# Products of zeros on TensorE in the idle time of its plan: into a spare bank up to the first block, into an open accumulator later

## The chip, the cores and the metric

The kernel runs on one core of a Trainium2 chip. The metric is the device time of one execution in microseconds (us); lower is better. TensorE does the matrix products, VectorE (DVE in the profile), ScalarE (ACT) and GpSimd (POOL) the rest, and SyncE (SP) issues the loads and stores.

## What is computed

Three stages follow each other: an attention by landmarks, a channel mixer behind a Fourier transform, and a gated mixer.

```python
q_lm = q.reshape(B, H, m, S // m, D).mean(axis=3)        # B 8, H 8, S 576, D 64, m 32
k_lm = k.reshape(B, H, m, S // m, D).mean(axis=3)
A, Bm, C = sm(q, k_lm), sm(q_lm, k_lm), sm(q_lm, k)      # sm: scaled softmax of a @ b.T
Z = Bm.T / (norm1(Bm) * norminf(Bm) + 1e-06)
for _ in range(6):
    Z = 2 * Z - Z @ Bm @ Z
x = A @ Z @ C @ v                                        # then heads side by side: 8 x 576 x 512
u = x + real(fft(fft(x, axis=1), axis=2))
un = (u - mean(u)) / sqrt(var(u) + 1e-06)
x = u + np.maximum(un @ w_ch1, 0.0) @ w_ch2              # 512 -> 2048 -> 512
xk, xr = mixes of x and of x one token back
k = np.maximum(xk @ w_k, 0.0)
out = sigmoid(xr @ w_r) * (k * k @ w_v)                  # 512 -> 1024 -> 512, 512 -> 512
```

## The kernel before

The tokens (8 batches of 576) are cut into nine blocks of 512 (`BLK`, `NB`). `phase1` (line 544) does the attention and the transform of one batch: `landmarks`, `chain_b` (with its `series` of six steps on the tiles `RX` and `bdR`), `chain_c`, `chain_a`, `tail`. Its products are small and mostly float32, and go into PSUM banks named `gp`. `norm` (line 1058) normalizes one block; its first two blocks take the sums of squares by 16 products of one column each, `one` with `tmp`, issued in two passes (x32 in the trace). `block_a` (line 1127) is the channel mixer of one block. Its `first(f)` (line 1133) makes 12 products of 512 columns into one of two banks `ph` and its `second(f)` (line 1148) makes 12, three each into four accumulators `acc`, banks 0 to 3, that stay open from f = 0 to f = 15. The order is first(0), then first(f), second(f-1) in turn, then second(15). The class `Gated` (after the loop at line 1187) does the third stage in the same way.

Each weight comes as 64-bit floats and is turned into two float16 halves on chip by `Weights.run`: three ScalarE steps and three VectorE steps on `wbits` or `more`, then a high half on ScalarE (`w1h`, `w2h`) and a low half on VectorE (`w1l`, `w2l`). Those of `block_a` are 32 pieces, put in among the batches and the first blocks.

Nothing is issued as the program text stands. Every call records an `Op` (line 128) with a cost in us, and `Plan.issue` (line 365) simulates the engines: each Op starts when its engine is free and its operands are there (with `HOP`, 0.2 us, from engine to engine), the one with the largest key (its path to the end plus its `lead`) first. PSUM banks are handed out in the same simulation by `grant` (line 421): `fixed` (line 387) holds the banks that are bound to `acc` and `ph` from the time that their first product could start, and `gp` takes any other. The order found is then issued engine by engine and stays as it is. A product costs its columns divided by 2400 plus 0.0025 us in the plan (line 315), float32 four times that and 0.17 at least, so the plan has TensorE at its higher clock all the time. The products of `block_a` and `Gated` have `chain=True`: they keep the order in which they were recorded.

Of the kernel before, what the change touches and what calls it, by code (L numbers as in the profile page):

```python
# [11 lines left out]
F32 = mybir.dt.float32  # L12
F16 = mybir.dt.float16
# [36 lines left out]
def wide(x):  # L50
    return int(np.prod(x.shape[1:]))


class Ref:


    def __init__(self, tile, view, path=()):
        self.tile, self.view, self.path = tile, view, path
        self.shape, self.dtype = view.shape, view.dtype
# [68 lines left out]
class Op:  # L128
    def __init__(self, index, eng, run, cost, port=False, nbytes=0):
        self.index, self.eng, self.run, self.cost = index, eng, run, cost  # L130
        self.port, self.nbytes = port, nbytes
        self.preds, self.succs = set(), []
        self.tail = self.lead = self.est = self.end = 0.0
        self.group = self.last = None

NOW, START, CONVERT, SOON = 1000.0, 400.0, 170.0, 200.0


class Engine:
# [44 lines left out]
class Plan:  # L187
# [6 lines left out]
    def __init__(self, nc, shadow):  # L194
        self.nc, self.shadow = nc, shadow
        self.ops, self.groups = [], []
        self.slots, self.turn = {}, {}
        self.lead = self.slack = 0.0
        self.chained, self.count = None, 0
        self.v = Engine(self, nc.vector, "v")  # L200
        self.s = Engine(self, nc.scalar, "s")
        self.g = Engine(self, nc.gpsimd, "g")
# [112 lines left out]
    def mm(self, out, lhsT, rhs, start, stop, chain=False, **kw):  # L315

        cost = wide(rhs) / 2400.0 + 0.0025
        if rhs.dtype == F32:
            cost = max(4 * cost, 0.17)
        share = 4 if wide(lhsT) <= 32 else 2 if wide(lhsT) <= 64 else 1  # L320

        def run():
            self.nc.tensor.matmul(  # L323
                out.real(), lhsT=lhsT.real(), rhs=rhs.real(), start=start, stop=stop, **kw
            )

        op = self.record("pe", run, cost / share, [out], [lhsT, rhs])
        if chain:
            op.lead = 0.0
            if self.chained:  # L330
                op.preds.add(self.chained)
            self.chained = op

    def tr(self, out, in_, ident):
        def run():
            self.nc.tensor.transpose(out.real(), in_.real(), ident.real())  # L336

        self.record("pe", run, 0.108, [out], [in_, ident])
# [26 lines left out]
    def issue(self):  # L365
        ops = self.ops
        for g in self.groups:
            if g.group[0].bank is None:
                g.preds = self.outside(g)
            else:  # L370
                g.preds = g.group[0].ops[0].preds - {g}
        for op in ops:
            for p in op.preds:
                p.succs.append(op)
        for op in reversed(ops):
            cost = op.cost + (op.nbytes / 340e3 + 2.0 if op.nbytes else 0.0)
            op.tail = cost + max([
                s.tail + (self.HOP if s.eng != op.eng and op.eng else 0.0) for s in op.succs
            ] or [0.0])
            op.key = op.tail + op.lead  # L380
        left = {op: len(op.preds) for op in ops}
        free = dict(pe=0.0, v=0.0, s=0.0, g=0.0, sp=0.0)
        later = {e: [] for e in free}
        avail = {e: [] for e in free}
        pending, order = [], []
        bank = {n: 0.0 for n in range(8)}
        fixed, holds = set(), {}
        port = dma = 0.0

        def ready(op):  # L390
            op.est = max(
                [0.0]
                + [
                    p.end + (self.HOP + op.slack if p.eng and p.eng != op.eng else 0.0)
                    for p in op.preds
                ]
            )
            if op.group:
                first = min((o for t in op.group for o in t.ops), key=lambda o: o.index)
                op.est = max([0.0] + [p.end for p in first.preds if p is not op])  # L400
                op.key = first.key
                pending.append(op)
                if op.group[0].bank is not None:
                    fixed.add(op.group[0].bank)
            elif op.eng is None:
                done(op, op.est)
            else:
                heapq.heappush(later[op.eng], (op.est, op.index, op))

        def done(op, end):  # L410
            op.end = end
            for t in holds.pop(op, ()):
                t.left -= 1
                if t.left == 0:
                    bank[t.bank] = max(o.end for o in t.ops) + self.HOP
            for s in op.succs:
                left[s] -= 1
                if left[s] == 0:
                    ready(s)

        def grant():

            best = None
            wanted = sorted(pending, key=lambda g: -g.key)
            for k, g in enumerate(wanted):
                if g.group[0].bank is not None:
                    got = [g.group[0].bank]
                else:
                    got = sorted(
                        (b for b in bank if b not in fixed and bank[b] < np.inf),  # L430
                        key=lambda b: bank[b],
                    )[:len(g.group)]
                    if len(got) < len(g.group):
                        continue
                t = max([g.est] + [bank[b] for b in got])
                if t < np.inf and (best is None or t < best[0]):
                    best = t, g, got
            return best

        for op in ops:  # L440
            if not op.preds:
                ready(op)
        while len(order) < sum(op.eng is not None for op in ops):
            when = []
            for e in free:
                if avail[e]:
                    when.append((free[e], e))
                elif later[e]:
                    when.append((max(free[e], later[e][0][0]), e))
            g = grant()  # L450
            if g and (not when or g[0] <= min(when)[0]):
                t, op, got = g
                pending.remove(op)
                for x, b in zip(op.group, got):
                    x.bank, x.left = b, len(x.ops)
                    bank[b] = np.inf
                    for o in x.ops:
                        holds.setdefault(o, []).append(x)
                done(op, t)
                continue  # L460
            t, e = min(when)
            while later[e] and later[e][0][0] <= t:
                x = heapq.heappop(later[e])[2]
                heapq.heappush(avail[e], (-x.key, x.index, x))
            op = heapq.heappop(avail[e])[2]
            start = max(t, port) if op.port else t
            free[e] = end = start + op.cost
            if op.port:
                port = end
            if op.nbytes:  # L470
                dma = max(dma, end) + op.nbytes / 340e3
                end = dma + 2.0
            op.begin = start
            order.append(op)
            done(op, end)
        self.order, self.span = order, max(op.end for op in order)
        for op in order:
            op.run()
# [477 lines left out]
def build(nc, tc, a):  # L956
    shadow = bacc.Bacc("TRN2", target_bir_lowering=False, num_devices=1)
    iss = Plan(nc, shadow)
    v_, s_, g_ = iss.v, iss.s, iss.g
    mm, tr = iss.mm, iss.tr  # L960
    stack, pa_stack, p1_stack = ExitStack(), ExitStack(), ExitStack()
    with stack, tc.manual_schedule():
        ps_pool = Pool(stack, tc, "ps", space=PSUM)
        com = Pool(stack, tc, "com")
# [28 lines left out]
        one = iss.tile(com, [128, 1], F32, "one")  # L993
        v_.memset(one, 1.0 / DM)
        ones = one.to_broadcast([128, 128])
        w1 = [iss.tile(pa, [128, 4, FF1], F16, f"w1{x}") for x in "hl"]
        w2 = [iss.tile(pa, [128, 16, DM], F16, f"w2{x}") for x in "hl"]
        weights = Weights(iss, com)
# [128 lines left out]
        def block_a(i, un):  # L1127
            u = ub[i]
            acc = acc_banks()
# [18 lines left out]
            def second(f):  # L1148
                h = hs.pop(f)
                for m in range(4):  # L1150
                    sl = slice(128 * m, 128 * m + 128)
                    for n, (x, y) in enumerate(PARTS):
                        mm(
                            acc[m], w2[x][:, f, sl], h[:, y], f == 0 and n == 0,
                            f == 15 and n == 2, chain=True,
                        )

            first(0)
            for f in range(1, 16):
# [167 lines left out]
        for n in range(8 * NB + 2):  # L1327
            i, f = divmod(n, 8)
# [96 lines left out]
```

## Time and profile before

| | |
|---|---|
| median of 3 runs | 1582.57 us (1581.19 to 1584.06) |
| the profiled execution | 1584.5 us, span 1582.7 us |
| TensorE busy | 1529.7 us, 97% of the span |
| VectorE, ScalarE, GpSimd busy | 883.9 us (56%), 600.5 us (38%), 288.4 us (18%) |
| mean granted TensorE clock | 0.978 |

The granted clock is the share of full speed that the chip lets TensorE have; it has two levels here, 1.00 (2.4 GHz) and 0.50 (1.2 GHz), and a window over both shows a mean. A busy TensorE is not always a fast one: at the lower level a product is busy for twice the time. "Idle before" in a timeline is the time in which the engine had nothing running ahead of that instruction, and the name behind the arrow is what ended it.

### The profile page before, as it was taken

To read this page: it belongs to the slowest core of one execution; us is meant where nothing else is said; L and a number is where in the kernel's file an instruction comes from. 1 tells how busy PE (TensorE), PEld (TensorE's weight loads), DVE (VectorE), ACT (ScalarE), POOL (GpSimd) and SP (SyncE) were. 2 spreads that over 40 slices of the span, in tenths; PEclk is the share of its full clock that TensorE was granted. 3 is DMA by queue.
4 is the path that set the end of the run, shared out by engine and by line. 5 is a ranking of instruction groups with operands and counts; after the bars stand their busy time and mean duration, and the time that the engine had idled before them with its cause. 6 is when DMAs were issued, how large, how long until landed. Compare 5 with 4: busy or idle time off the path is not lost.

```text
span 1582.7 us, 20918 instructions
## 1 busy us (share of the span) xinstructions
PE 1529.7 (97%) x8182; PEld 784.4 (50%) x8182; DVE 883.9 (56%) x1802; ACT 600.5 (38%) x1233; POOL 288.4 (18%) x347
## 2 busy tenths in 40 slices
PE   6879899999999999999999999999999999999998
PEld 5535455555564554554544444444444444444443
DVE  6798887776764764634515344211587766643222
ACT  4465654444433433322312123111655544443221
POOL 2012020221210210210102012000454533221100
PEclk8788899999999999999999999999999999999999
DMA  7243414132322222100002200000121011000000
GB/s 272 67 133 121 134 55 152 38 115 76 100 71 81 86 72 80 61 1 28 1 0 80 107 28 0 27 0 28 53 80 54 27 54 54 28 1 27 27 28 27
DMA packets 43587, 97.87 MB, mean 62 GB/s; under 512 B 4064, under 2 KB 9440, under 8 KB 42976
## 3 DMA queue, kind: packets, MB, share of 16 engines
q1 hardware_dynamic: 43488, 96.53, 17.8%
q8 instruction: 65, 1.06, 0.3%
q14 instruction: 34, 0.28, 0.1%
HBM read 72.39 MB, written 24.12 MB: 61 GB/s over the span
## 4 chain that ended last, share of the span: by engine, by line
PE 93%; DVE 4%; ACT 1%; issue 1%; DMA 0%; SPq 0%; POOL 0%; ACTq 0%; DVEq 0%
PE ph L323 35%; PE acc L323 35%; PE gp L323 21%; PE gp L336 2%; DVE wbits L180 1%; DVE more L180 0%; DVE small L180 0%; DMA k<-in_k 0%; DVE uc L180 0%; DVE w1l L180 0%; DVE h L180 0%; ACT h L180 0%; DVE d L180 0%; DVE un L180 0%; DVE w2l L180 0%
## 5 line engine op out<-in xcount | busy, mean ns | idle before, releaser
L323 PE MATMUL ph<-un,w1h 128*128 128x512 f16 x1152 | 353.6, 382 | 10.6 <-DVE bst L180 6.1
L323 PE MATMUL acc<-h,w2h 128*128 128x512 f16 x1152 | 350.8, 382 | 1.2 <-ACT w2h L180 1.2
L180 DVE SCALAR_TENSOR_TENSOR h<-ph,h 128x512 f16<-128x512 f32 x144 | 99.3, 690 | 283.2 <-ACT h L180 282.4
L180 ACT ACTIVATE h<-ph 128x512 f16<-128x512 f32 x144 | 85.9, 597 | 379.2 <-PE ph L323 378.7
L323 PE MATMUL acc<-h,w2l 128*128 128x512 f16 x576 | 219.8, 382 | 4.3 <-DVE w2l L180 4.3
L323 PE MATMUL ph<-un,w1l 128*128 128x512 f16 x576 | 219.8, 382 | 3.1 <-DVE w1l L180 3.1
L323 PE MATMUL ph<-xk,w_k 128*128 128x512 f16 x864 | 199.6, 379 | 0.0
L323 PE MATMUL acc<-w_v,k 128*128 128x512 f16 x864 | 198.9, 379 | 0.0
L323 PEld LDWEIGHTS <-w1h 128*128 128x128 f16 x1152 | 113.0, 99 | 138.4 <-issue 14.5
L323 PEld LDWEIGHTS <-w2h 128*128 128x128 f16 x1152 | 113.6, 99 | 131.6 <-issue 8.8
L180 DVE TENSOR_TENSOR rk<-rk 128x512 f32<-128x512 f32 x72 | 55.5, 770 | 146.3 <-ACT rk L180 145.9
L323 PEld LDWEIGHTS <-k 128*128 128x128 f16 x864 | 84.6, 98 | 100.6
L323 PEld LDWEIGHTS <-w_k 128*128 128x128 f16 x864 | 84.5, 98 | 99.7
L323 PE MATMUL gp<-w_r,xr 128*128 128x512 f16 x432 | 99.3, 379 | 0.7 <-ACT rs L180 0.7
L180 DVE SCALAR_TENSOR_TENSOR wbits<-wst,wbits 128x512 int32<-128x512 int32 x132 | 94.4, 731 | 2.8 <-ACT wbits L180 1.6
L180 ACT ACTIVATE rk<-ph 128x512 f32<-128x512 f32 x72 | 43.0, 597 | 129.2 <-PE ph L323 121.6
L323 PEld LDWEIGHTS <-w2l 128*128 128x128 f16 x576 | 57.1, 99 | 69.9 <-DVE w2l L180 5.3
L323 PEld LDWEIGHTS <-w1l 128*128 128x128 f16 x576 | 57.1, 99 | 68.6 <-DVE w1l L180 4.6
L180 DVE TENSOR_TENSOR k<-rk,k 128x512 f16<-128x512 f32 x72 | 59.3, 823 | 29.3 <-ACT k L180 29.1
L180 POOL TENSOR_TENSOR sq<-sq 128x513 f32<-128x513 f32 x27 | 36.6, 1356 | 198.7 <-ACT sq L180 198.1
L180 POOL TENSOR_TENSOR xr<-xt,xr 128x512 f16<-128x512 f32 x36 | 48.6, 1375 | 112.1 <-ACT xr L180 112.0
L323 PEld LDWEIGHTS <-xr 128*128 128x128 f16 x432 | 42.2, 98 | 51.4 <-issue 0.9
(156 smaller groups left out, 1977.3 us busy)
## 6 DMA issues: line engine op xcount, KB each, us to landing
wst<-in_w_ch SPq DMA_DIRECT2D x24, 512.0 KB, 4.0
q<-in_q SPq DMA_DIRECT2D x16, 578.0 KB, 5.1
k<-in_k SPq DMA_DIRECT2D x16, 576.0 KB, 4.6
ys<-ub SPq DMA_DIRECT2D x36, 256.0 KB, 2.1
out<-o SPq DMA_DIRECT2D x36, 256.0 KB, 2.0
yb<-ys SPq DMA_DIRECT2D x8, 1026.0 KB, 5.3
v<-in_v SPq DMA_DIRECT2D x8, 1024.0 KB, 5.6
more<-in_w_ch SPq DMA_DIRECT2D x8, 512.0 KB, 4.4
```

The costliest lines, as they stand in the source:

```text
L180: f(real(out), *map(real, args), **{k: real(x) for k, x in kw.items()})
L323: self.nc.tensor.matmul(out.real(), lhsT=lhsT.real(), rhs=rhs.real(), start=start, stop=stop, **kw)
L336: self.nc.tensor.transpose(out.real(), in_.real(), ident.real())
```

## The change

The simulation in `Plan.issue` now looks at every Op that it gives to TensorE. If the engine was idle in the plan ahead of it, a number of extra products, int((idle - 0.15) / 0.3), is put into TensorE's queue ahead of that Op. Each multiplies a column of zeros, read again and again as a 128x128 and a 128x512 operand, so it is a product of 512 columns. Up to the first product of the chain (first(0) of block 0, that one included) they go to a bank that nothing else uses, bank 3 (`WARM`), each as a product of its own. From the start of a block's accumulator 3 to the product ahead of its last one they are added to that accumulator, where they add zero. Between these stretches, from the chain's first product to the opening of block 0's accumulator 3, between blocks, and in the whole third stage, none is put in. Bank 3 is in `fixed` from the start, so `gp` has seven banks instead of eight before the first block. The zeros are written by a memset on GpSimd with the highest lead, and idle time counts from its end. The loop's end condition is rewritten for the same meaning, and extra products take no time in the simulation.

```diff
+WARM = 3
@@ Plan.mm
             if self.chained:
                 op.preds.add(self.chained)
+            else:
+                self.first_chained = op
             self.chained = op
+        return op
@@ Plan.issue
-        fixed, holds = set(), {}
+        fixed, holds = {WARM}, {}
         port = dma = 0.0
+        warming = []
...
             start = max(t, port) if op.port else t
+            was = free[e]
             free[e] = end = start + op.cost
...
             op.begin = start
+            if e == "pe" and (not warming or warming[-1] is not None):
+                into = warming[-1] if warming else None
+                idle = start - max(was, self.warm_from.end)
+                order += [
+                    Op(0, "warm", partial(self.warm, into), 0.0)
+                ] * int((idle - 0.15) / 0.3)
+            if op is self.first_chained:
+                warming.append(None)
+            if op.opens is not None:
+                warming.append(op.opens)
+            if op.closes:
+                warming.append(None)
             order.append(op)
@@ build
+        zero = iss.tile(com, [128, 2], F16, "zero")
+        iss.lead = NOW
+        iss.warm_from = g_.memset(zero, 0.0)
+        iss.lead = START
+        spare = []
+
+        def warm(into):
+            if not spare:
+                spare.append(ps_pool.get().tile(
+                    [128, 512], F32, tag=f"bank{WARM}", name="spare", bufs=1
+                ))
+            z = zero.real()[:, 0:1]
+            nc.tensor.matmul(
+                into.real() if into else spare[0], lhsT=z.to_broadcast([128, 128]),
+                rhs=z.to_broadcast([128, 512]), start=not into, stop=not into,
+            )
+
+        iss.warm = warm
@@ block_a, second
-                        mm(
+                        op = mm(
                             acc[m], w2[x][:, f, sl], h[:, y], f == 0 and n == 0,
                             f == 15 and n == 2, chain=True,
                         )
+                        if m == 3 and f == 0 and n == 0:
+                            op.opens = acc[3]
+                        if m == 3 and f == 15 and n == 1:
+                            op.closes = True
```

## Rows read from the trace of the kernel before

**Rows 1.** The page: busy us, share of the span and instructions of each engine.

```profile
PE 1529.7 (97%) x8182; PEld 784.4 (50%) x8182; DVE 883.9 (56%) x1802; ACT 600.5 (38%) x1233; POOL 288.4 (18%) x347
```

**Rows 2.** The chain that ended last: shares by engine, then one piece (start, us, what).

```profile
PE 93%; DVE 4%; ACT 1%; issue 1%; DMA 0%; SPq 0%; POOL 0%; ACTq 0%; DVEq 0%
...
215.74 2.59 PE ph L323 x12
```

**Rows 3.** Windows: length, then PE, PEld, DVE, ACT, POOL busy, granted clock, DMA.

```profile
9.07:20.27 11.20, 11.20 (x60) 9.16 (x61) 5.63 (x10) 1.26 (x2) 0.61 (x1) 1.00 1.05 367
...
30.51:51.00 20.49, 18.63 (x82) 14.13 (x83) 14.78 (x44) 9.36 (x31) 7.07 (x10) 0.50 0.29 91
68.06:85.13 17.07, 9.88 (x39) 7.50 (x40) 13.69 (x33) 8.17 (x14) 0.00 (x0) 0.50 0.11 36
115.85:126.09 10.24, 6.98 (x20) 2.10 (x21) 9.84 (x27) 7.18 (x15) 1.75 (x2) 0.50 0.33 107
149.98:153.39 3.41, 3.41 (x17) 2.13 (x15) 3.41 (x7) 1.95 (x4) 0.51 (x1) 0.50 0.34 85
170.46:173.87 3.41, 3.41 (x17) 2.72 (x18) 3.24 (x9) 1.96 (x4) 0.00 (x0) 0.50 0.51 159
184.11:190.94 6.83, 5.99 (x15) 2.15 (x16) 6.54 (x18) 3.15 (x5) 0.00 (x0) 0.50 0.48 143
228.49:231.90 3.41, 3.41 (x12) 1.06 (x11) 2.99 (x15) 0.99 (x3) 0.67 (x1) 0.50 0.00 0
```

**Rows 4.** Timeline of PE: start, us, operation, count, and [idle before and what ended it].

```profile
9.07 6.80 PE L323 MATMUL gp<-kbd,q 128*97 128x64 f32 x40 [9.07 <-POOL kbd L180]
15.79 4.16 PE L323 MATMUL gp<-k,qbd 128*64 128x288 f32 x14
...
67.45 6.46 PE L323 MATMUL gp<-one,tmp 128*128 128x1 f32 x32 [1.52 <-ACT tmp L180]
...
93.78 2.88 PE L323 MATMUL gp<-kbd,q 128*97 128x64 f32 x32
...
127.69 1.19 PE L323 MATMUL gp<-k,qbd 128*64 128x288 f32 x8
...
224.84 3.63 PE L323 MATMUL gp<-one,tmp 128*128 128x1 f32 x32
```

**Rows 5.** Waits of PE, 0 to 82 us: us in total, times, longest; first and last.

```profile
PE gp L323 <- POOL kbd L180: 9.1, 1, 9.1
...
PE gp L336 <- DVE bst L180: 0.2, 1, 0.2
```

**Rows 6.** Waits of PE, 83 to 250 us: first and last of eleven kinds.

```profile
PE ph L323 <- DVE bst L180: 6.1, 1, 6.1
...
PE gp L323 <- ACT acs L180: 0.4, 1, 0.4
```

**Rows 7.** Timeline of PE: two long waits ahead of products of block 0, and one before.

```profile
76.64 1.12 PE L336 MATMUL gp<-ident,small 128*128 128x128 f32 x4 [2.73 <-DVE small L180]
82.22 1.01 PE L323 MATMUL ph<-un,w1h 128*128 128x512 f16 x2 [4.47 <-ACT wbits L180]
...
118.11 1.03 PE L323 MATMUL ph<-un,w1h 128*128 128x512 f16 x2 [6.14 <-DVE bst L180]
```

**Rows 8.** Windows cut where the chain changes engine; columns as in the group of windows above.

```profile
21.30:46.00 24.70, 20.24 (x164) 15.82 (x163) 18.13 (x69) 15.50 (x46) 8.58 (x11) 0.62 0.43 157
46.00:55.53 9.53, 8.96 (x37) 5.11 (x36) 5.96 (x10) 4.53 (x15) 0.68 (x2) 0.74 0.57 166
66.06:82.20 16.14, 7.58 (x36) 7.10 (x37) 12.79 (x33) 8.92 (x16) 0.00 (x0) 0.56 0.20 65
82.00:250.00 168.00, 144.78 (x802) 76.43 (x803) 143.82 (x303) 98.18 (x202) 26.31 (x31) 0.91 0.36 118
250.00:450.00 200.00, 199.92 (x1341) 115.87 (x1340) 138.51 (x348) 81.06 (x207) 36.95 (x45) 1.00 0.28 92
```

**Rows 9.** Timeline of POOL: what the products k,qbd of batch 0 read.

```profile
11.49 0.61 POOL L180 TENSOR_TENSOR qbd<-qs,c_mask 128x256 f32<-128x256 f32 x1 [2.48 <-DVE qs L180]
```

More of the change, by code (lines that the diff above doesn't have):

```diff
@@ L133, in __init__ @@
         self.tail = self.lead = self.est = self.end = 0.0
-        self.group = self.last = None
+        self.group = self.last = self.opens = self.closes = None
 NOW, START, CONVERT, SOON = 1000.0, 400.0, 170.0, 200.0
+WARM = 3
 class Engine:
@@ L199, in __init__ @@
         self.chained, self.count = None, 0
+        self.warm = None
         self.v = Engine(self, nc.vector, "v")
@@ L442, in issue @@
                 ready(op)
-        while len(order) < sum(op.eng is not None for op in ops):
+        while any(avail.values()) or any(later.values()) or pending:
             when = []
@@ L473, in issue @@
             op.begin = start
+            if e == "pe" and (not warming or warming[-1] is not None):
[10 more added lines that the diff above has]
+                warming.append(None)
             order.append(op)
             done(op, end)
+        assert all(not n for n in left.values())
         self.order, self.span = order, max(op.end for op in order)
```

## The prediction

> **What bounds the kernel now.** I read the page first: TensorE is busy for 97% of the span [rows 1], and the chain that ended last runs on it for 93% [rows 2]. So the sum of TensorE's work, at the clock it is granted, and its waits is the time. After 250 us there is nothing left to win: from 250 to 450 us it is busy for 199.92 of 200 us at granted clock 1.00, with VectorE at 69% [rows 8]. What is lost is lost before.
>
> Next, windows cut where the granted clock changes [rows 3]. Seven stretches are at 0.50, the lower level (1.2 GHz). The one from 9.07 to 20.27 us is printed with 1.00, but I count it as low too: 40 products kbd,q take 6.80 us in it and 32 of them 2.88 us at 93.78, which is 0.17 against 0.09 us each, and the 14 products k,qbd at 15.79 take 0.30 each against 0.15 at 127.69 [rows 4]. TensorE is busy in these eight stretches for 62.9 us (11.20 + 18.63 + 9.88 + 6.98 + 3.41 + 3.41 + 5.99 + 3.41). At the upper level the same work takes half, so **31.5 us** is the most that a better clock can give. A page of the Trainium skill bears on this size: "TensorE: Matmul & The Clock Gate" (Part 1, What's actually happening) says that the ramp penalty is under 1% of a typical kernel's span, which would be 15.8 us here. The windows show twice that, because the clock falls again and again; by the page the gain could not pass 15.8 us, which is about what I come to for another reason.
>
> Third, the waits of TensorE. Up to 82 us there are ten, 18.3 us in all, of which 9.1 is the start [rows 5]; another of 4.47 stands right ahead of the first product of block 0 [rows 7]. From 83 to 250 us there are fourteen, 22.7 us in all, the longest 6.14 [rows 6, 7]. After the long ones the clock is found at the lower level [rows 3, 7]. But it also falls without a wait: at 228.49 [rows 3], just after 32 products of one column that keep TensorE "busy" from 224.84 for 3.63 us [rows 4]. The plan counts those as work, so no zeros go in there.
>
> Last, who would hold the chain if TensorE were faster: VectorE. It is busy for 86% of the stretch from 82 to 250 us (143.82 of 168) [rows 8]. In the low stretches at 115.85, 149.98, 170.46 and 184.11 us it is at 95 to 100% [rows 3].
>
> **Part by part. The zeros themselves.** A product of 512 columns takes 0.216 us at the upper level (12 in 2.59 us [rows 2]) and 0.43 at the lower. The plan puts one in for each 0.3 us of idle time beyond the first 0.15, so at the upper level they fill at most 72% of the idle time that the plan sees and cost nothing: they lie in TensorE's own waits. At the lower level they take 1.43 times the idle time and run over. If the plan saw the waits of the trace, it would put in about 29 at the start ((9.07 - 0.15) / 0.3), 8 and 14 into the waits of 2.73 and 4.47 us [rows 7], some 15 into the rest before, and some 60 after 83 us: 127. It counts TensorE at the upper level throughout, so it sees up to 31.5 us more idle time, at most 105 more. That makes 127 to 232 products, 27 to 50 us of TensorE's time. No trace row shows a product with such repeated operands, or what zeros do to the clock. I take 0.216 and 0.43, since every product of 512 columns here takes that, and treat the clock as a rival.
>
> **The start.** 29 products from about 1 us on, at the lower level until the clock rises. The dense work of block 0 that starts at 82.22 sees its rise at 85.13, that at 184.95 at 190.94 [rows 3, 7], so 3 to 6 us: at 5 us, 12 products at 0.43 and 17 at 0.216 end at 1 + 5 + 3.7 = 9.7. The first real product was free at 9.07 [rows 5], so 0.6 us is lost (between 0 and 1.7). Then kbd,q takes 40 x 0.09 = 3.6 us instead of 6.80. The products k,qbd, ready when GpSimd's qbd ends at 12.10 [rows 9], end at about 14.9 instead of 20.1. I book **-5.2**, and the 0.6 against it.
>
> **Up to block 0.** From 21.3 to 46 us VectorE has 18.13 us of work in 24.70, from 46 to 55.5 it has 5.96 in 9.53 [rows 8]. TensorE at double speed would pull more, but VectorE's share here is taken to reach the 86% that it holds later: 21.2 and 7.0 us, **-3.5** and **-2.5** (at 100%, -6.6 and -3.6; at the present share, 0). From 66 to 82 the 32 one-column products take 3.63 instead of 6.46 if the clock is high when they begin [rows 4]; -2.8 less 0.8 for zeros that run over in the waits of 2.73 and 4.47 us, since the clock falls after such products: **-2.0**. The first 2.9 us of block 0 are low now [rows 3, 7]: **-1.4**. Against it: bank 3 is taken from gp. all waits up to 82 us name an operand, none plainly a bank [rows 5]. After 83 us, where gp has only two banks, the mean wait is 22.7 / 14 = 1.6 us [rows 6]; with seven of eight I take +0.5 (-1.6 to 1.6, since another order can by chance be the shorter). And I put +1.5 for one stretch in which the clock falls all the same, among the narrow products of the series. Sum to here: -14.6 + 0.6 + 0.5 + 1.5 = **-12.0**.
>
> **From block 0 to 250 us.** Half of the low busy time is 3.5, 1.7, 1.7, 3.0 and 1.7 us [rows 3]. VectorE has little room: over 115.85 to 150 it can give 2.3, over 150 to 174 some 0.5, over 174 to 228 some 2.0, and the one at 228.49 stays: **-4.8** (between 0 and -9.9). Zeros cost here where the queue reaches them with the next operand already there, since TensorE takes its queue in order and the real product, with VectorE or ScalarE behind it, waits: some 60 products, 13 us at 0.216. I take a tenth of them on the chain, **+1.5** (0 to 13).
>
> **The rest.** One memset of two columns on GpSimd, ahead of its part of kbd, for which TensorE waits until 9.07 us [rows 5] and which itself waits for k: nothing. No DMA is added or moved, and SP's queue keeps its order. After 250 us the plan should see hardly any idle time, as the trace doesn't [rows 8]: nothing.
>
> Sum: -12.0 - 4.8 + 1.5 = -15.3 us. From the profiled execution, 1584.5, that gives 1569.2. The median of the runs shown is 1.9 us below that execution, so the median after comes to 1567.
>
> **Rivals.**
> (a) VectorE takes nearly all: only the start (-5.2) and a little more are kept, and VectorE's chain of weight pieces ends last from 30 us on. For it: its 95 to 100% in the late low stretches. Against it: 6.6 us free in the 24.7 from 21.3 [rows 8]. -7: 1576.
> (b) VectorE gives way: the plan was made for the upper level, so its order fits once the clock is there, and nearly all of the 31.5 but the last stretch is kept, less 2 of overrun: -28, 1554. Against it: the same 95%.
> (c) Slower: the zeros of the blocks stand ahead of operands that are there already. The place is the queue between 83 and 250 us, the price 0.216 each, 0.43 while the clock is low. With 60 to 110 products, most of them on the chain, that is 13 to 24 us against the 5 of the start and little else: +8 to +16, about 1592. It decides as soon as TensorE runs some 1 us or more behind its plan there, so that a planned wait of usual size (22.7 / 14 = 1.6 us) is gone.
> (d) The change doesn't do what it says: products of zeros don't raise the clock. Then they run over: 29 x 0.43 = 12.5 from 1 us on, 4.4 us over; 22 x 0.43 = 9.5 in 7.2 us, 2.3 over; about 4 for all others. +11: 1593.
> (e) It evens out within 0.2%: 1582.
>
> **Chances.** Forecast 0.50 (its own range 1559 to 1573); (a) 0.16; (b) 0.15; (c) 0.08; (d) 0.05; (e) 0.06. A run of this kernel can tell about 0.2%, 3.2 us, from no change. Faster: 0.50 + 0.16 + 0.15 = 0.81; same 0.06; slower 0.13. The range reaches from (b) to the end of (a): 1551 to 1580, leaving out (c), (d) and (e), 0.19.
>
> **What the profile would show.** Right: 512-column products from the first microseconds, kbd,q at 0.09 each, the lower level nearly gone before 82 us, ph's first product at about 70, VectorE at 86% or more from 21 us on, and the same dense rhythm from about 235 us to the end. Wrong: a granted clock of 0.50 beside rows of zeros (d); TensorE busy without a break between 83 and 250 us while the real products come later (c); unchanged waits for wbits, w1l and w2l with more idle time on TensorE (a). The forecast fails most easily at VectorE's 86%, which is a share carried from one stretch to another.

## The result and the profile after

The changed kernel takes 1560.92 us (1559.95 to 1563.39, four runs), the kernel before 1581.88 us beside it (1580.83 to 1584.06): 21.0 us less, a ratio of 0.9868 with a 95% interval of 0.9851 to 0.9885. The profiled execution of after took 1559.95 us, its span is 1558.2. The two profiled spans differ by 24.5 us, more than the medians, because the one of before was the slowest of its runs and the one of after the fastest.

The page of after, its first two parts and its chain. Busy time, share and instructions of each engine; the granted clock by slices of a fortieth; the chain that ended last.

```profile
PE 1545.3 (99%) x8386; PEld 787.4 (51%) x8386; DVE 883.2 (57%) x1802; ACT 600.8 (39%) x1233; POOL 288.7 (19%) x348
...
PEclk9999999999999999999999999999999999999999
...
PE 95%; DVE 4%; ACT 1%; issue 0%; DMA 0%; ACTq 0%; POOL 0%; DVEq 0%; POOLq 0%
```

TensorE has 204 products more than in [rows 1], and the granted clock is 0.9 or more in every slice. All products of zeros, by where they go:

```profile
L1031 PE MATMUL acc<-zero 128*128 128x512 f16 x120 | 29.3, 381 | 0.0
L1031 PE MATMUL spare<-zero 128*128 128x512 f16 x84 | 23.9, 431 | 0.9 <-POOL zero L184 0.9
```

The order of all other instructions is the same as before on each of the five queues, but for one place: a product of block 0 (ph with un and w1h) stands ahead of eight small products ks,qbd at 85.12 us, where before it stood behind them at 101.92. These eight take 0.42 us together. So little but the zeros, the memset and the places of the banks can have moved the time.

TensorE's timeline of after, at the places of [rows 4] and [rows 7]:

```profile
0.89 8.76 PE L1031 MATMUL spare<-zero 128*128 128x512 f16 x29 [0.89 <-POOL zero L184]
9.49 3.67 PE L328 MATMUL gp<-kbd,q 128*97 128x64 f32 x40
13.10 2.21 PE L328 MATMUL gp<-k,qbd 128*64 128x288 f32 x14
...
59.17 3.09 PE L1031 MATMUL spare<-zero 128*128 128x512 f16 x9
62.05 1.10 PE L344 MATMUL gp<-ident,small 128*128 128x128 f32 x4
62.94 2.00 PE L1031 MATMUL spare<-zero 128*128 128x512 f16 x7
64.78 0.38 PE L328 MATMUL ph<-un,w1h 128*128 128x512 f16 x1
...
108.95 1.19 PE L328 MATMUL gp<-k,qbd 128*64 128x288 f32 x8
...
201.82 3.63 PE L328 MATMUL gp<-one,tmp 128*128 128x1 f32 x32
```

The 29 zeros at the start are the 29 of the prediction; the last of them hold the first real product back to 9.65 us (by the chain), and from there the 40 products kbd,q take 0.09 us each. Block 0 begins at 64.78 instead of 82.22 us, the half of k,qbd that stood at 127.69 stands at 108.95, and the one-column products that stood at 224.84 stand at 201.82 [rows 4, 7].

Windows of after, answering to [rows 8] (length, then PE, PEld, DVE, ACT, POOL busy, granted clock, DMA):

```profile
16.58:36.30 19.72, 18.99 (x194) 12.78 (x194) 18.30 (x69) 15.41 (x46) 9.07 (x11) 1.00 0.78 294
36.30:42.93 6.63, 6.07 (x33) 3.54 (x32) 5.85 (x11) 4.54 (x15) 0.68 (x2) 1.00 0.61 169
54.02:69.46 15.44, 13.40 (x70) 7.74 (x69) 14.64 (x35) 9.42 (x16) 0.00 (x0) 0.89 0.19 67
72.00:232.00 160.00, 158.59 (x1008) 86.44 (x1007) 144.50 (x308) 99.86 (x206) 27.38 (x32) 1.00 0.38 128
225.00:425.00 200.00, 199.92 (x1341) 115.75 (x1339) 138.87 (x349) 80.63 (x205) 36.88 (x45) 1.00 0.28 93
```

The first two are the stretches that were 24.70 and 9.53 us long. VectorE's work in them is the same as before (18.30 and 5.85 us against 18.13 and 5.96); the time around it is what shrank. From 225 us on, the kernel is the old one, moved forward.

The waits of TensorE after 83 us (engine, product, what ended the wait: us in total, times, longest), all of them to the end:

```profile
PE gp L344 <- DVE small L184: 1.1, 2, 0.6
PE gp L328 <- ACT rs L184: 0.7, 1, 0.7
PE acc L328 <- DVE w2l L184: 0.6, 1, 0.6
PE gp L328 <- DVE RX L184: 0.4, 1, 0.4
PE gp L328 <- DVE A L184: 0.2, 1, 0.2
```

3.0 us are left up to the end, 1.2 of them (w2l, RX and A) before 250 us, of what was 22.7 between 83 and 250 us [rows 6]: zeros stand where the waits were.

### The profile page after: what moved, and what is told of

The parts are those of the page before. It is cut to its first block, busy times and chain, and to the rows that moved or that the text cites. A ratio compares the mean times of both kernels' runs of the same rounds, so it can differ in the third digit from the quotient of the medians.

```text
span 1558.2 us, 21327 instructions
## 1 busy us (share of the span) xinstructions
PE 1545.3 (99%) x8386; PEld 787.4 (51%) x8386; DVE 883.2 (57%) x1802; ACT 600.8 (39%) x1233; POOL 288.7 (19%) x348
## 4 chain that ended last, share of the span: by engine, by line
PE 95%; DVE 4%; ACT 1%; issue 0%; DMA 0%; ACTq 0%; POOL 0%; DVEq 0%; POOLq 0%
PE ph L328 35%; PE acc L328 35%; PE gp L328 21%; PE gp L344 2%; PE spare L1031 1%; PE acc L1031 1%; DVE small L184 1%; DVE wbits L184 1%; DVE more L184 0%; DVE sm L184 0%; DVE d L184 0%; DVE bst L184 0%; DVE h L184 0%; DVE cst L184 0%; DVE A L184 0%
```

## The experiments

**One stretch alone.** The changed kernel with products into the spare bank alone:

```diff
-            if e == "pe" and (not warming or warming[-1] is not None):
+            if e == "pe" and not warming:
```

> The changed kernel with the 84 products into the spare bank alone, none into the accumulators; the plan and the order of all else stay. Theory (the gain is the clock on real work, and the two stretches add up): block 0 starts about 16.4 us earlier than before and that is kept, while the low stretches after it come back; the median is about 1566 (16 below before). Rival 1 (VectorE's chain of weight pieces after 80 us takes back what is won ahead of it): 1573 or more. Rival 2 (the gain is made in the blocks): 1578 or more.

Measured: 1569.37 us, ratio 0.9917 (0.9903 to 0.9931), 12.2 below before, where 16 were expected. And with products into the accumulators alone:

```diff
-            if e == "pe" and (not warming or warming[-1] is not None):
+            if e == "pe" and warming and warming[-1] is not None:
```

> The changed kernel with the 120 products into the accumulators alone, none before the first block. Theory: block 0 starts as before, at about 82 us; from there to 250 us some 5 us are won, so that this and the run with the spare bank alone add up to the whole change; the median is about 1577. Rival 1 (VectorE holds the blocks whatever the clock): 1581 to 1582, no gain. Rival (zeros stand on the chain and cost more than the clock gives): 1584 or more.

Measured: 1575.18 us, ratio 0.9949 (0.9931 to 0.9968), 6.4 below, where 5 were expected, with single runs from 1566.15 to 1577.01. Each stretch gives a part by itself, the one ahead of block 0 about twice as much as the other, and the rivals (nearly all of it taken back later, all of it made in the blocks, zeros that cost more than they give) fall. 12.2 and 6.4 are 18.6 of 21.0, and what the bank alone gives (the next run) counts in both. But the three intervals are 4 to 6 us wide, so it isn't shown that the two stretches give more together than by themselves.

In the profile with the spare bank alone the first product into an accumulator starts at 72.57 us, 16.3 earlier than before, and 14.5 of that are left at the end: a little is taken back. The clock is still low in the blocks. The same window as above, of that kernel:

```profile
72.00:232.00 160.00, 138.25 (x768) 74.50 (x766) 135.54 (x290) 94.44 (x195) 26.24 (x31) 0.89 0.36 115
```

0.89 is no better than the 0.91 that the kernel before has from 82 to 250 us [rows 8]. Fewer real products fit into the same 160 us, and VectorE does less too.

**No zeros at all.** The bank and the memset stay.

```diff
-                ] * int((idle - 0.15) / 0.3)
+                ] * 0
```

> The changed kernel without any product of zeros: bank 3 kept from gp and the memset are all that is left of the change. Theory: the order of the real work is the same as before on all engines, so 1581 to 1583, within 0.1% of before. Rival (the bank, by the physical places of gp, is part of the gain or a cost under it): more than 3 us off before, either way.

Measured: 1579.82 us, ratio 0.9991 (0.9982 to 1.0000): 1.8 us below before, between nothing and 2.8; a little below the 1581 to 1583 expected, and short of the rival's 3 us. So the bank costs nothing, and may give a little. One place in the trace could be the cause. TensorE's first products of block 0 in this kernel:

```profile
74.53 0.59 PE L328 MATMUL ph<-un,w1h 128*128 128x512 f16 x1 [1.44 <-ACT un L184]
75.67 0.58 PE L328 MATMUL ph<-un,w1h 128*128 128x512 f16 x1 [0.55 <-DVE un L184]
```

They wait for un, 1.44 and 0.55 us. Before, the first waited 4.47 us [rows 7], although it reads the same tile in the same order. From the products ident,small to the first product into an accumulator it takes 10.5 us (71.98 to 82.50) instead of 12.2 (76.64 to 88.82), 1.7 less. On VectorE of before stands, just ahead of that start at 82.22:

```profile
81.40 0.68 DVE L180 SCALAR_TENSOR_TENSOR uc<-uc,gp 128x512 f32<-128x512 f32 x1
```

It reads a gp bank, and it ends at 82.08. With bank 3 out of gp's reach, other banks are handed out, and it may be that the first product no longer has to wait for this one. That the bank is the cause is argued from these rows, not shown by a run of its own.

**Without the start.** The 29 products ahead of the first real product are left out, the other 175 stay.

```diff
-            if e == "pe" and (not warming or warming[-1] is not None):
+            if e == "pe" and was and (not warming or warming[-1] is not None):
```

> The changed kernel without the 29 products ahead of the very first real product; the other 175 stay. Theory: the first real products run at the lower level again, from 9.07 us to about 20, and the 4.6 us that the start gave are lost and not made up later: median about 1565.5, 4.6 above the changed kernel. Rival (VectorE's later chain absorbs them): 1561 to 1562.

Measured: 1566.30 us, ratio 0.9904 (0.9892 to 0.9917), 5.4 above the changed kernel, near the 4.6 expected. Its TensorE begins as the kernel before does:

```profile
8.63 6.80 PE L328 MATMUL gp<-kbd,q 128*97 128x64 f32 x40 [8.63 <-POOL kbd L184]
```

0.17 us each instead of 0.09. What the start gives at 20 us, it still gives at 1560: nothing later absorbs it.

**How many.** One product for each 0.6 us of planned idle time in the blocks instead of each 0.3 (56 instead of 120), then one for each 0.15 (248), then one for each 0.4 (86); the 84 of the spare bank stay.

```diff
-                ] * int((idle - 0.15) / 0.3)
+                ] * int((idle - 0.15) / (0.6 if into else 0.3))
```

> The changed kernel with 56 instead of 120 products into the accumulators (one for each 0.6 us of planned idle time); the 84 into the spare bank stay. Theory (a tenth of the zeros stand on the chain, 1.5 us, and the clock holds with half of them): about 1 us faster than the changed kernel, 1560, with the granted clock still near 0.999. Rival 1 (the clock needs them): the lower level comes back between 83 and 250 us, 1563 to 1566. Rival 2 (most zeros of the blocks stand on the chain, 10 us by the chain of the changed kernel): 1555 to 1557.

Measured: 1563.02 us, ratio 0.9877 (0.9863 to 0.9890), 2.1 above the changed kernel: not the 1560 expected, but the first rival's 1563 to 1566, and the lower level is back in its profile (102.4 to 105.8 and 204.8 to 211.6 us).

> The changed kernel with 248 instead of 120 products into the accumulators (one for each 0.15 us of planned idle time). 128 more of 0.216 us are 27.6 us of TensorE time; the planned waits hold about 0.3 us for each of the 120, 36 us plus 0.15 for each wait. Theory (each real wait is about the planned one, so twice the zeros run over by 0.13 us for each planned 0.3): 53.6 us of zeros in some 40 us of waits, 10 to 15 us on the chain, median 1571 to 1576. Rival 1 (VectorE holds the chain, TensorE has room): 1561 to 1564. Rival 2 (waits of TensorE are already full, each more stands on the chain): 27 us, 1588.

Measured: 1586.77 us, ratio 1.0031 (1.0018 to 1.0044): slower than before.

> The changed kernel with 86 instead of 120 products into the accumulators (one for each 0.4 us of planned idle time). So far 0, 56, 120 and 248 of them gave 1569.4, 1563.0, 1560.9 and 1586.8. Theory (two slopes: fewer zeros let the clock fall, more stand on the chain at 0.2 us each, and the turn lies between 56 and 120): 1559 to 1561, at best 2 us below the changed kernel, with a mean granted clock of 0.997 or more. Rival (the clock alone counts up to 120, the zeros being free): on the line between 56 and 120, about 1562.

Measured: 1561.88 us, ratio 0.9869 (0.9849 to 0.9889): the rival's 1562, outside the 1559 to 1561 of the theory, but not to be told from the changed kernel. A best number between 56 and 120 isn't seen.

| products into the accumulators | 0 | 56 | 86 | 120 | 248 |
|---|---|---|---|---|---|
| median, us | 1569.4 | 1563.0 | 1561.9 | 1560.9 | 1586.8 |

The same window of the kernels with 56, 86 and 248, in this order:

```profile
72.00:232.00 160.00, 147.84 (x858) 79.16 (x857) 142.13 (x304) 98.91 (x204) 26.51 (x31) 0.97 0.38 129
```

```profile
72.00:232.00 160.00, 152.75 (x889) 82.10 (x888) 142.23 (x306) 99.23 (x205) 26.70 (x31) 0.98 0.38 129
```

```profile
72.00:232.00 160.00, 160.00 (x940) 87.17 (x939) 125.47 (x271) 88.72 (x182) 24.39 (x29) 1.00 0.33 109
```

From 0 to 56 the granted clock of the window goes from 0.89 to 0.97, and some 6 us are won. From 56 to 120 it goes 0.97, 0.98, 1.00, and the medians fall by 2.1 us more, but that is within the scatter: single runs reach from 1562.87 to 1564.98, from 1559.14 to 1562.94 and from 1559.95 to 1563.39. Up to the one-column products the three kernels run alike. With 56 and with 86:

```profile
201.74 4.03 PE L328 MATMUL gp<-one,tmp 128*128 128x1 f32 x32
201.37 4.25 PE L328 MATMUL gp<-one,tmp 128*128 128x1 f32 x32
```

With 120 they start at 201.82 us. What sets the three windows apart stands mostly behind these products, 6.8 us at the lower level with 56 and 86, and there the clock also falls, for 3.4 us, in the profile of the kernel without the start, which has all 120. So it is shown that 56 hold the clock better than none, not that 120 hold it better than 56.

From 120 on TensorE is full, and nearly each further product stands on the chain: 25.9 us for 128 of them, 0.20 us each, nearly the 0.216 that one takes. VectorE then waits for TensorE (125.47 us busy against 144.50). My expectation of 10 to 15 us for the run with 248 fell to its second rival: after 120 products there is no room left.

**Who else holds the chain.** VectorE's third bit step of each weight piece does one column instead of 512; part of the weights' bits is left out, the plan's costs, its order and the zeros stay.

```diff
         v_.scalar_tensor_tensor(
-            bits, high, -0x40000000, bits, op0=ALU.bitwise_and, op1=ALU.bitwise_or
+            bits, high, -0x40000000, bits, narrow=True, op0=ALU.bitwise_and, op1=ALU.bitwise_or
         )
...
+                if narrow:
+                    f(real(out)[:, 0:1], real(args[0])[:, 0:1], args[1], real(args[2])[:, 0:1], **kw)
+                    return
```

In the changed kernel:

> The changed kernel with VectorE's third bit step of each of the 52 weight pieces cut from 512 columns to 1 (0.69 to about 0.06 us each): the weights are wrong in their sign and exponent bits, and 32 x 0.6 = 19 us of VectorE's work before about 225 us are left out; plan, order and zeros stay. Theory (VectorE sets the chain in much of the blocks once the clock is up): 6 to 10 us below the changed kernel, 1551 to 1555, bounded by the zeros, whose number was planned with the whole work. Rival (TensorE alone sets it): within 2 us of the changed kernel.

Measured: 1559.55 us, ratio 0.9854 (0.9840 to 0.9867), 1.4 below the changed kernel: as the rival had it, not the 6 to 10 of the theory. The step on one column takes 0.16 us in this trace, not about 0.06, so some 0.53 us of each piece are left out, 17 us in 32 pieces. In the kernel before:

> The kernel before with the same cut of VectorE's third bit step (part of the weights' bits is left out). Theory (before the change TensorE's low clock held part of the chain, so VectorE's work counts for less): 4 to 8 us below before, 1574 to 1578, less than the same cut gives in the changed kernel. Rival (VectorE set the chain before as much as after): the same difference in both, within 1.5 us.

Measured: 1578.57 us, ratio 0.9971 (0.9960 to 0.9982), 3.5 below before, a little less than the 4 to 8 expected. The theory wanted less here than in the changed kernel; with intervals of 3 to 5 us, 3.5 and 1.4 can't be told apart. In the changed kernel with 56 products in the blocks:

> The changed kernel with VectorE's third bit step of each weight piece cut to one column (part of the weights' bits is left out) and with only 56 of the 120 products into the accumulators; plan and order stay. With all 120 the cut gave next to nothing (1559.6), and TensorE was then busy for 149.4 of 150 us from 72 to 222. Theory (VectorE sets when operands come, and the zeros, 0.2 us each, stood where its earlier operands could have gone in): the 64 zeros that are gone, 13.8 us, let the cut through: 1550 to 1556. Rival (VectorE was not the bound; zeros and their clock weigh against each other as with the whole bit step, where half the zeros gave 1563.0): 1560 to 1564.

Measured: 1557.06 us, ratio 0.9836 (0.9820 to 0.9853), 6.0 below the same kernel with the whole step (1563.02). The window of the changed kernel with the cut, and then the one-column products in it and in the kernel with the cut and 56 products:

```profile
72.00:222.00 150.00, 149.43 (x876) 81.83 (x875) 118.69 (x284) 93.03 (x193) 24.36 (x30) 0.98 0.36 122
...
200.60 4.68 PE L331 MATMUL gp<-one,tmp 128*128 128x1 f32 x32
...
196.00 4.10 PE L331 MATMUL gp<-one,tmp 128*128 128x1 f32 x32
```

VectorE's share falls to 79%, and TensorE stays full, with zeros where earlier operands could have gone in; the one-column products start 1.2 us earlier than without the cut. Take 64 zeros away and they start 5.7 us earlier (196.00 against 201.74), and 6 us of the cut come through in the time, just outside the 1550 to 1556 expected and nearer to it than to the rival's 1560. So VectorE does set when real operands come, and the number of zeros, planned from VectorE's whole work, sets when TensorE takes them: both hold the chain at once.

The same cut, known to the plan, so that it is made anew:

> The changed kernel with the same bit step cut to one column in the plan too, so that the plan and its order are made anew and see less idle time (73 products into the spare bank and 27 into the accumulators; part of the weights' bits is left out). Theory (VectorE sets the chain in the blocks once the clock is up): with 19 us less of VectorE's work before about 225 us, real waits shrink by 10 us or more: 1545 to 1552. Rival (TensorE's own work sets it): 1556 to 1560.

Measured: 1566.50 us, ratio 0.9898 (0.9883 to 0.9913).

> The kernel before with the bit step cut to one column in the plan too (part of the weights' bits is left out). Theory (TensorE's low clock held part of the chain before the change): 6 to 10 us below before, 1572 to 1576, a smaller difference than the same cut gives in the changed kernel. Rival (VectorE held the chain before already, as much as after): 12 us or more below before, 1570 or less.

Measured: 1570.58 us, ratio 0.9923 (0.9908 to 0.9937). The first missed both of its ranges (1545 to 1552 and 1556 to 1560), the second came out at its rival's bound. They settle nothing on the question. The new plan puts only 27 products into the accumulators, the first of them at 185.4 us, and the clock of the changed kernel is low for much of the time before that:

```profile
75.00:230.00 155.00, 140.24 (x779) 77.51 (x779) 119.29 (x285) 91.69 (x195) 26.03 (x30) 0.88 0.35 113
```

That is about the granted clock of the kernel without zeros in the blocks (0.89). The second shows only that with a plan made for it, the cut is worth 12 us in the kernel before.

## Why the prediction was right, and where its sum was off

The forecast was 1567 us, 15.3 us won; 21.0 were, inside the range and inside the forecast's own 1559 to 1573. The mechanism is the one forecast. The clock rises under products of zeros, which ends (d): kbd,q runs at 0.09 us each behind the first 29, and up to 232 us the clock of after falls only once, near 60 us (0.89 from 54.02 to 69.46). Without any zeros nothing or little is won (0 to 2.8 us). TensorE is busy for 158.59 of 160 us in the blocks, nearly without a break as (c) had it, and 120 zeros went in there, more than the forecast's 60 and (c)'s 60 to 110; but the real products come earlier (the one-column ones at 201.82 instead of 224.84), not later, which ends (c). The run with 248 products shows (c) at work, with its price right (0.20 us each). (a) and (e) end by the 21.0. Rival (b), VectorE gives way, came in part: 21.0 lies about halfway between the forecast and its 28, and VectorE's room is one of the terms that the sum had too small.

The prediction counts eight low stretches. There is a ninth, inside a window of before that shows a mean:

```profile
23.68:27.10 3.42, 3.42 (x51) 2.48 (x51) 3.32 (x8) 2.98 (x9) 1.98 (x3) 0.50 1.04 406
```

With it the low busy time is 66.3 us instead of 62.9, and 33.2 could be won instead of 31.5; 21.0 are somewhat under two thirds of that. The 15.8 us that the prediction has as a bound from 1% of the span were passed.

Term by term, the times of the same instruction before and after, in the two profiled executions. The chain's first reductions cst and the first products into an accumulator, before and after:

```profile
20.11 1.19 DVE cst L180 x3
15.39 1.19 DVE cst L184 x3
...
88.82 0.59 PE L323 MATMUL acc<-h,w2h 128*128 128x512 f16 x2
72.48 0.59 PE L328 MATMUL acc<-h,w2h 128*128 128x512 f16 x2
```

- **The start**, booked at 4.6 net: the cst reductions begin at 15.39 us instead of 20.11, 4.7. Leaving the start out costs 5.4. Right, with the 29 products and their run-over of 0.6 us.
- **21 to 46 us**, booked at 3.5: the stretch takes 19.72 us instead of 24.70, so 5.0. The step that was mis-sized is the cap of 86% on VectorE's share. It reached 93% (18.30 of 19.72).
- **46 to 55.5 us**, booked at 2.5: 2.9; VectorE at 88% (5.85 of 6.63).
- **55.5 to 66 us**, booked at nothing: 0.6 lost (11.09 us instead of 10.53). Three zeros stand on the chain there for 0.65 us, between products of 512 columns.
- **66 us to the first accumulator**, booked at 2.0 and 1.4: 2.6 and 1.7, cut where the same uc of VectorE ends (82.08 before, 67.47 after).
- **The bank**, booked at 0.5 lost, and **one relapse of the clock**, booked at 1.5 lost: the bank cost nothing (1.8 won, 0 to 2.8), and no relapse came among the products of the series; the one near 60 us follows the first one-column products. With the cap these are most of the 4.3 us by which the first part was too small: 16.3 instead of 12.0.
- **The blocks**, booked at 3.3 net: 8.2, of which 2.4 up to the second half of k,qbd, 4.3 from there to the one-column products, and 1.5 behind them. The first agrees with the 2.3 booked. The second was to be 0.5 up to 174 us and 2.0 behind; the 2.0 came, and instead of the 0.5 came 2.3 (the two windows below). The third was booked at nothing, as a stretch that stays low; in the profiled execution of after the clock didn't fall there. The 1.5 booked against these for zeros on the chain can't be told apart from them.

```profile
148.97:175.00 26.03, 22.14 (x142) 14.81 (x143) 24.66 (x43) 17.96 (x39) 2.34 (x5) 0.87 0.32 103
130.30:154.00 23.70, 23.52 (x164) 14.70 (x165) 23.22 (x41) 18.07 (x40) 2.45 (x4) 1.00 0.35 113
```

These are the same stretch before and after. VectorE was busy for 95% of it and is now for 98%, and 1.4 us of its work have moved out of it. So a high share was no sign there that it had nothing to give.

That the clock did not fall at the one-column products near 205 us looks like luck. Of the nine profiles of kernels with zeros in the blocks, it falls in seven at the end of these products or just behind them, for 3.4 to 6.8 us; the other two are that of after and that with 248 products. The runs of the changed kernel at 1561.8 and 1563.4 have a mean granted clock of 0.997, the two at 1560.0 have 0.999, so it may have fallen in those two as well. So a part of the 24.5 us between the two profiles is the luck of those two executions, and the medians are the better measure: by them the mis-sized steps are 5.7 us together.

What stays open is what the bank does, and whether the two stretches give more together (21.0 us) than by themselves (18.6). No run tells it.

## What to carry to other kernels

Look for time in which the busiest engine is busy at a low clock; here that was 66.3 us of busy time in nine stretches of the first 232 us. Work without effect pays as long as it lies inside waits that are really there: 56 products in the blocks won some 6 us and 120 some 8, which can't be told apart, and the next 128 lost 25.9. And after such a filling the next gain isn't found by making the other engine faster alone, since the filling holds the place (1.4 us with 120 products, 6.0 with 56); the two have to be changed together, and a new plan with less filling can lose the clock again (0.88 with 27).

## What the runs showed that I had not expected

- A share of 86% was no bound for VectorE. With the operands there in time it was busy for 93% of 19.72 us and 90% of 160 us, in an order that nobody changed.
- Taking one bank of eight away from the small products did no harm, and the first products of block 0 waited 1.44 and 0.55 us instead of 4.47.
- The number of products that the plan's idle time gave fitted the real waits well: 120 products left 3.0 us of waits after 83 us, and the next 128 were on the chain almost in full.
- The clock can fall at products of one column, although TensorE is busy with them without a break: before, from 224.84 to 228.47 us, and it is at 0.50 from 228.49 [rows 3, 4]. With zeros in the blocks it still falls at the same products in seven of nine profiles.
